# Attention tiles with tokens on partitions and DMA transposes in a fused linear-attention and two-layer kernel

## The chip, the cores and the metric

One core of one Trainium2 chip. The metric is the device time of one execution in microseconds (us). A run over 1.5% above the fastest of its kernel is marked slow. Ratios are the mean time of one kernel's fast runs over the mean of the other's fast runs of the same rounds, so they are not quite the ratio of the medians quoted.

## The reference, cut to what matters

```python
# batch 8, heads 8, seq 576, head_dim 64; d_model 512, d_ff 2048
kv  = einsum('bhsd,bhse->bhde', k, v)        # 64 x 64 per head
out = einsum('bhsd,bhde->bhse', q, kv)
x   = out / sqrt(mean(out*out, -1) + 1e-6) * g_norm   # per head; then [4608 tokens, 512]
h   = x @ w_in                                # [4608, 2048]
g   = max(h, 0) + alpha * min(h, 0)
y   = g @ w_out                               # [4608, 512]
```

The two-layer part works on nine blocks of 512 tokens, the attention on eight batches of 576.

## The kernel before: the parts that matter

Everything runs as one hand-ordered stream per engine. Block w computes the first layer of block w (64 matmuls of 512 columns in 16 groups), the second layer of block w-1 (another 64), and, between the groups, the attention of block w+1. Each head pair j takes five transposes of q on TensorE, five matmuls for kv, then:

```python
def step_ot(w, j):          # out, transposed: 128 columns of d_model x 512 tokens
    ... nc.tensor.matmul(out=ot_ps[...], lhsT=kvs[b, j][:], rhs=qts[b, j][...])
    nc.scalar.activation(out=sq[:], in_=ot_ps[:], func=AF.Square)
def ssq_mm(w, j):           # sum of squares over a head's 64 partitions: a matmul with a mask
    nc.tensor.matmul(out=ssq_ps[:], lhsT=mask16[:], rhs=sq[:])
    ... Ln, then Exp on 128 x 512, on ScalarE
def norm(w, j):             # x, transposed, ready as the moving operand of the first layer
    nc.vector.scalar_tensor_tensor(out=xts[w, j][:], in0=ot_ps[:], scalar=g2col[:], in1=rstd[:], ...)
```

Loads of a batch are issued from GpSimd (six DMAs: remainder and main part of k, v, q), and GpSimd then regroups k and q in SBUF. At block w the loads are of batch w+2, which block w+1 uses:

```python
        if 1 < w and w + 2 < B:
            load_batch(w + 2)       # at the start of block w
            regroup_batch(w + 2)
        for g in range(NF):
            m1_group(w, g)          # 4 matmuls of the first layer, Relu on ScalarE, gt on VectorE
            ...                     # 4 matmuls y of the second layer
            ...                     # some attention steps of block w + 1
```

In the profiles h_ps is the first layer, y_ps the second, qt_ps the q transposes, gt the activated values; kst, vst, qst are the staging tiles of the loads and ksb, qsb the regrouped ones. A DMA lands when its data have arrived. A PSUM bank is the buffer that a group of matmuls writes into; groups that share one take turns (at the end of block 1 of the changed kernel two groups of kv matmuls waited 0.86 and 1.06 us until VectorE had copied the one before out of their bank).

## Time and profile before

| | |
|---|---|
| time, median of 3 | 320.28 us (318.98 to 320.32) |
| span of the profiled run | 317.4 us |
| busy: TensorE / ScalarE / VectorE / GpSimd | 92% / 55% / 50% / 21% |
| granted TensorE clock | 0.993 |

A line of the profile's groups and timelines gives engine, source line, operation, out<-in, shape and count; a bracket tells how long the engine stood idle just before and what ended that. TensorE's busy time is modelled to the end of each matmul and overlaps the next (a matmul of 512 columns counts 0.379 us, and one starts every 0.216), so I measure prices and gaps from one start to the next. The lines themselves stand in the prediction below.

### The profile page before, as it was taken

To read this page: it belongs to the slowest core of one execution; us is meant where nothing else is said; L and a number is where in the kernel's file an instruction comes from. 1 tells how busy PE (TensorE), PEld (TensorE's weight loads), DVE (VectorE), ACT (ScalarE), POOL (GpSimd) and SP (SyncE) were. 2 spreads that over 40 slices of the span, in tenths; PEclk is the share of its full clock that TensorE was granted. 3 is DMA by queue.
4 is the path that set the end of the run, shared out by engine and by line. 5 is a ranking of instruction groups with operands and counts; after the bars stand their busy time and mean duration, and the time that the engine had idled before them with its cause. 6 is when DMAs were issued, how large, how long until landed. Compare 5 with 4: busy or idle time off the path is not lost.

```text
span 317.4 us, 4195 instructions
## 1 busy us (share of the span) xinstructions
PE 293.4 (92%) x1588; PEld 142.0 (45%) x1588; DVE 157.2 (50%) x267; ACT 173.4 (55%) x292; POOL 66.6 (21%) x74
## 2 busy tenths in 40 slices
PE   5668998898999999999999999999999999999994
PEld 1323453454455455545554455444544444444441
DVE  4547833666655554545464546454554445443300
ACT  2366546468466636674567456655665667444211
POOL 8434312737340541055005200000000000000000
PEclk9799999999999999999999999999999999999999
DMA  7999999998973859077715811000011111001132
GB/s 110 179 206 195 200 197 143 174 149 89 169 101 51 115 92 118 34 104 113 108 35 86 120 35 33 33 36 33 33 35 33 33 33 36 33 34 37 52 80 66
DMA packets 47621, 28.27 MB, mean 89 GB/s; under 512 B 14304, under 2 KB 42992, under 8 KB 47600
## 3 DMA queue, kind: packets, MB, share of 16 engines
q0 software_dynamic: 40320, 18.16, 45.7%
q1 hardware_dynamic: 7280, 9.84, 11.2%
q8 instruction: 12, 0.20, 0.3%
q14 instruction: 9, 0.07, 0.1%
HBM read 36.71 MB, written 9.44 MB: 145 GB/s over the span
## 4 chain that ended last, share of the span: by engine, by line
PE 85%; ACT 6%; DVE 4%; DMA 2%; issue 1%; SPq 1%; ACTq 0%
PE h_ps L323 37%; PE y_ps L345 36%; PE qt_ps L234 3%; PE kv_ps L249 3%; PE ssq_ps L287 3%; PE ot_ps L271 2%; DMA alpha_row<-in_moe_alpha_dram 2%; ACT rstd L289 2%; ACT sq_sb L277 1%; ACT rstd L292 1%; DVE gt L332 1%; DVE xt L298 1%; ACT m_sb L330 1%; SPq L100 1%; PE yb L345 1%
## 5 line engine op out<-in xcount | busy, mean ns | idle before, releaser
L332 DVE SCALAR_TENSOR_TENSOR gt<-m_sb,beta_sb,h_ps 128x512 f16<-128x512 f32 x144 | 106.8, 745 | 87.2 <-ACT m_sb L330 86.4
L323 PE MATMUL h_ps<-xt,w_in_sb 128*128 128x512 f16 x576 | 146.2, 379 | 2.9 <-DVE xt L298 1.7
L345 PE MATMUL y_ps<-w_out_sb,gt 128*128 128x512 f16 x528 | 134.8, 379 | 0.1
L330 ACT ACTIVATE m_sb<-h_ps 128x512 f32<-128x512 f32 x144 | 85.3, 594 | 80.4 <-PE h_ps L323 80.3
L345 PEld LDWEIGHTS <-gt 128*128 128x128 f16 x576 | 56.1, 98 | 67.1 <-issue 1.7
L323 PEld LDWEIGHTS <-w_in_sb 128*128 128x128 f16 x576 | 54.2, 98 | 64.2 <-issue 10.4
L298 DVE SCALAR_TENSOR_TENSOR xt<-ot_ps,g2col,rstd 128x512 f16<-128x512 f32 x36 | 27.0, 751 | 43.3 <-ACT rstd L292 43.2
L289 ACT ACTIVATE rstd<-ssq_ps,eps_t 128x512 f32<-128x512 f32 x36 | 24.7, 687 | 18.0 <-PE ssq_ps L287 17.9
L277 ACT ACTIVATE sq_sb<-ot_ps 128x512 f16<-128x512 f32 x36 | 21.3, 596 | 16.2 <-PE ot_ps L271 15.6
L352 ACT COPY y_sb<-y_ps 128x512 f32<-128x512 f32 x33 | 19.3, 586 | 18.4 <-PE y_ps L345 18.4
L292 ACT ACTIVATE rstd<-rstd 128x512 f32<-128x512 f32 x36 | 22.7, 629 | 1.1
L287 PE MATMUL ssq_ps<-sq_sb,mask 128*128 128x512 f16 x36 | 13.6, 378 | 6.7 <-ACT sq_sb L277 5.6
L129 POOL DMA_DIRECT2D vst<-in_v_dram x9 | 7.7, 860 | 50.4 <-PE kv_ps L249 48.6
L146 POOL COPY qsb<-qst 128x2048 f16<-128x2048 f16 x6 | 11.4, 1897 | 32.5 <-DMA qst<-in_q_dram 32.5
L249 PEld LDWEIGHTS <-ksb 128*128 128x128 f16 x160 | 11.6, 99 | 11.2 <-issue 4.2
L234 PE MATMUL qt_ps<-ident,qsb 128*128 128x128 f16 x160 | 14.4, 225 | 1.9 <-DVE qsb L146 1.2
L234 PEld LDWEIGHTS <-qsb 128*128 128x128 f16 x160 | 11.6, 101 | 9.4 <-DVE qsb L146 2.4
L243 DVE COPY qt_sb<-qt_ps 128x576 f16<-128x576 f16 x32 | 14.4, 451 | 2.5 <-PE qt_ps L234 2.5
L271 PE MATMUL ot_ps<-qt_sb,kv_sb 128*128 128x512 f16 (+7 forms) x64 | 13.5, 286 | 0.8 <-DVE kv_sb L257 0.7
L249 PE MATMUL kv_ps<-vst,ksb 128*128 128x128 f16 x128 | 12.3, 220 | 1.8 <-DVE qt_sb L243 1.8
L146 POOL COPY ksb<-kst 128x2048 f16<-128x2048 f16 x6 | 11.4, 1903 | 11.9 <-DMA kst<-in_k_dram 11.9
L257 DVE TENSOR_TENSOR kv_sb<-kv_ps,mask 128x128 f16<-128x128 f32 x32 | 9.0, 285 | 3.8 <-PE kv_ps L249 3.8
(43 smaller groups left out, 92.6 us busy)
## 6 DMA issues: line engine op xcount, KB each, us to landing
out_dram<-y_sb SPq DMA_DIRECT2D x40, 128.0 KB, 2.4
out_dram<-y_sb SPq DMA_DIRECT2D x16, 256.0 KB, 2.3
kst<-in_k_dram POOLq DMA_DIRECT2D x7, 512.0 KB, 6.9
qst<-in_q_dram POOLq DMA_DIRECT2D x7, 512.0 KB, 10.1
vst<-in_v_dram POOLq DMA_DIRECT2D x7, 512.0 KB, 8.4
w_in_sb<-in_moe_w_in_dram POOLq DMA_DIRECT2D x4, 512.0 KB, 14.7
w_out_sb<-in_moe_w_out_dram POOLq DMA_DIRECT2D x4, 512.0 KB, 16.1
qst<-in_q_dram POOLq DMA_DIRECT2D x2, 256.0 KB, 7.5
```

Source lines behind the costliest of these rows:

```text
L146: (eng or nc.vector).tensor_copy(out=dst, in_=src)
L234: nc.tensor.matmul(out=qt_ps[:, t * P : (t + 1) * P], lhsT=qs(t), rhs=ident16[:], is_transpose=True, start=(t == 0), stop=(t == NT - 1),)
L249: nc.tensor.matmul(out=kv_ps[:], lhsT=ks(t), rhs=vs(t), start=(t == 0), stop=(t == NT - 1),)
L277: nc.scalar.activation(out=sq[:], in_=ot_ps[:], func=AF.Square)
L287: nc.tensor.matmul(out=ssq_ps[:], lhsT=mask16[:], rhs=sq[:], start=True, stop=True)
L289: nc.scalar.activation(out=rstd[:], in_=ssq_ps[:], func=AF.Ln, bias=eps_t[:], scale=inv_d,)
L292: nc.scalar.activation(out=rstd[:], in_=rstd[:], func=AF.Exp, bias=0.0, scale=-0.5)
L298: nc.vector.scalar_tensor_tensor(out=xts[w, j][:], in0=ot_ps[:], scalar=g2col[:], in1=rstd[:], op0=ALU.mult, op1=ALU.mult,)
L323: nc.tensor.matmul(out=h_ps[:], lhsT=w_in_blk(c, g), rhs=xts[w, c][:], start=(c == 0), stop=(c == NC - 1),)
L330: nc.scalar.activation(out=m_sb[:], in_=h_ps[:], func=AF.Relu, scale=-1.0)
L332: nc.vector.scalar_tensor_tensor(out=gt[:], in0=m_sb[:], scalar=beta_sb[:, g : g + 1], in1=h_ps[:], op0=ALU.mult, op1=ALU.add,)
L345: nc.tensor.matmul(out=y[:], lhsT=gts[w, g][:, a * P : (a + 1) * P], rhs=w_out_blk(g), start=(g == 0), stop=(g == NF - 1),)
```

## The change

Its intent is to take work off TensorE. From batch 3 on, q is transposed by a DMA; the attention's output is computed with tokens on partitions, so that the sum of squares is a reduction along the free axis on VectorE rather than a matmul; each normalised row tile is transposed back by a DMA into the first layer's operand `xm`. Row tiles and their transposes stand in groups 0 to 8 of a block; loads, then q transpose and kv, stand in groups 8 to 15.

```diff
+    def transpose_q(b):
+        qtms[b] = attn_p.tile([P, NT * NPAIR, P], FP16, name="qtm")
+        nc.sync.dma_start_transpose(out=qtms[b][:], in_=bufs[b % NBUF]["q"][:]...)
+    def tile_a(b, t):      # 128 tokens: four matmuls of 128 columns, Square on ScalarE
+    def tile_b(b, t):      # sum of squares: tensor_reduce on VectorE
+    def tile_c(b, t):      # Ln, Exp on 128 x 8; rg = rstd * g_norm on GpSimd
+    def tile_d(b, t):      # x = out * rg on VectorE, then
+            nc.sync.dma_start_transpose(out=xm(w)[:, :, c : c + m], in_=x[i : i + m]...)
...
+    LOAD_G = NF // 2
     for w in range(1, NW):
-        if 1 < w and w + 2 < B:
-            load_batch(w + 2)
-            regroup_batch(w + 2)
         for g in range(NF):
+            if w > 1 and g == LOAD_G and w + 2 < B:
+                load_batch(w + 2)
+                regroup_batch(w + 2)
             m1_group(w, g)
...
+            if g == NF - 3 and w + 2 < B:
+                transpose_q(w + 2)
+            if g >= NF - NPAIR and w + 2 < B:
+                step_kv(w + 2, g - (NF - NPAIR))
```

Cut: pools, the tail of batch 2 in the old layout, the scheduling of steps.

More of the change, by code (lines that the diff above doesn't have):

```diff
@@ L48 @@
     inv_d = 1.0 / D
+    NB_PE = 3
     const_p = ctx.enter_context(tc.tile_pool(name="constp", bufs=1))
     w_p = ctx.enter_context(tc.tile_pool(name="weights", bufs=1))
-    xt_p = ctx.enter_context(tc.tile_pool(name="xt", bufs=3))
+    xt_p = ctx.enter_context(tc.tile_pool(name="xt", bufs=2))
+    xm_p = ctx.enter_context(tc.tile_pool(name="xm", bufs=3))
     qkv_p = ctx.enter_context(tc.tile_pool(name="qkv", bufs=1))
@@ L60 @@
     ps_s = ctx.enter_context(tc.tile_pool(name="pss", bufs=1, space=bass.MemoryType.PSUM))
-    ps_o = ctx.enter_context(tc.tile_pool(name="pso", bufs=2, space=bass.MemoryType.PSUM))
-    ps_q = ctx.enter_context(tc.tile_pool(name="psq", bufs=1, space=bass.MemoryType.PSUM))
+    ps_o = ctx.enter_context(tc.tile_pool(name="pso", bufs=1, space=bass.MemoryType.PSUM))
     ctx.enter_context(
@@ L104 @@
     nc.sync.dma_start(out=alpha_row[:], in_=moe_alpha[:].rearrange("(g p) -> g p", p=P))
+    g_all = const_p.tile([P, D], FP32, name="g_all")
+    nc.sync.dma_start(out=g_all[:], in_=g_norm[:].partition_broadcast(P))
     g2col = const_p.tile([P, 1], FP32, name="g2col")
@@ L260, with xt_of @@
     ots = {}
+    xms = {}
+    def xt_of(w, c):
+        return xms[w][:, c, :] if w >= NB_PE else xts[w, c][:]
     def step_ot(w, j, pool=None):
@@ L265, in step_ot @@
         else:
-            ot_ps = ps_o.tile([P, W], FP32, name="ot_ps", tag="o")
+            ot_ps = ps_o.tile([P, W], FP32, name="ot_ps", tag=f"o{j % 2}")
         n0 = w * W
@@ L285, in ssq_mm @@
         ot_ps, sq = ots.pop((w, j))
-        ssq_ps = ps_q.tile([P, W], FP32, name="ssq_ps", tag="q")
+        ssq_ps = ps_o.tile([P, W], FP32, name="ssq_ps", tag="o2")
         nc.tensor.matmul(out=ssq_ps[:], lhsT=mask16[:], rhs=sq[:], start=True, stop=True)
@@ L301, in norm, with step_tail_ot @@
         )
+    TAIL = NB_PE * (S - W)
+    JT = min(NPAIR, W // TAIL)
+    def step_tail_ot(i):
+        ot_ps = ps_o.tile([P, JT, TAIL], FP32, name="ot_ps", tag=f"o{i % 2}")
+        for u in range(JT):
+            j = i * JT + u
+            nc.tensor.matmul(
+                out=ot_ps[:, u, :], lhsT=kvs[NB_PE - 1, j][:],
+                rhs=qts[NB_PE - 1, j][:, S - TAIL : S], start=True, stop=True,
+            )
+        sq = attn_p.tile([P, JT, TAIL], FP16, name="sq_sb")
+        nc.scalar.activation(out=sq[:], in_=ot_ps[:], func=AF.Square)
+        ots["tail", i] = (ot_ps, sq)
@@ new lines, in step_tail_ssq @@
+    def step_tail_ssq(i):
+        ot_ps, sq = ots.pop(("tail", i))
+        ssq_ps = ps_o.tile([P, JT, TAIL], FP32, name="ssq_ps", tag="o2")
+        nc.tensor.matmul(out=ssq_ps[:], lhsT=mask16[:], rhs=sq[:], start=True, stop=True)
+        rstd = attn_p.tile([P, JT, TAIL], FP32, name="rstd")
+        nc.scalar.activation(
+            out=rstd[:], in_=ssq_ps[:], func=AF.Ln, bias=eps_t[:], scale=inv_d,
+        )
+        nc.scalar.activation(out=rstd[:], in_=rstd[:], func=AF.Exp, bias=0.0, scale=-0.5)
+        nc.vector.scalar_tensor_tensor(
+            out=xm(NB_PE)[:, i * JT : (i + 1) * JT, 0:TAIL], in0=ot_ps[:], scalar=g2col[:],
+            in1=rstd[:], op0=ALU.mult, op1=ALU.mult,
+        )
@@ new lines, with xm @@
+    qtms, tiles = {}, {}
+    def xm(w):
+        if w not in xms:
+            xms[w] = xm_p.tile([P, NPAIR, W], FP16, name="xm")
+        return xms[w]
+    def transpose_q(b):
+        qtms[b] = attn_p.tile([P, NT * NPAIR, P], FP16, name="qtm")
+        nc.sync.dma_start_transpose(
+            out=qtms[b][:], in_=bufs[b % NBUF]["q"][:].rearrange("p t h d -> p (t h d)"),
+        )
+    n_tile = [0]
+    def tile_a(b, t):
+        u = n_tile[0] % 4
+        n_tile[0] += 1
+        pool, tag = (ps_o, f"o{u}") if u < 3 else (ps_s, "s")
+        ot_ps = pool.tile([P, H, D], FP32, name="otm_ps", tag=tag)
+        for j in range(NPAIR):
+            nc.tensor.matmul(
+                out=ot_ps[:, 2 * j : 2 * j + 2, :], lhsT=qtms[b][:, t * NPAIR + j, :],
+                rhs=kvs[b, j][:], start=True, stop=True,
+            )
+        n = P if t < TPP else REM
+        sq = attn_p.tile([P, H, D], FP32, name="sqm_sb", tag="rstd")
+        nc.scalar.activation(out=sq[0:n], in_=ot_ps[0:n], func=AF.Square)
+        tiles[b, t] = [n, ot_ps, sq]
@@ new lines, in tile_b @@
+    def tile_b(b, t):
+        n, _, sq = tiles[b, t]
+        ss = attn_p.tile([P, H], FP32, name="ss", bufs=3)
+        nc.vector.tensor_reduce(
+            out=ss[0:n], in_=sq[0:n], op=ALU.add, axis=mybir.AxisListType.X,
+        )
+        tiles[b, t][2] = ss
+    def tile_c(b, t):
+        n, _, ss = tiles[b, t]
+        nc.scalar.activation(
+            out=ss[0:n], in_=ss[0:n], func=AF.Ln, bias=eps_t[0:n], scale=inv_d,
+        )
+        nc.scalar.activation(out=ss[0:n], in_=ss[0:n], func=AF.Exp, bias=0.0, scale=-0.5)
+        rg = attn_p.tile([P, H, D], FP32, name="rg")
+        nc.gpsimd.tensor_tensor(
+            out=rg[0:n], in0=ss[0:n].unsqueeze(2).to_broadcast([n, H, D]),
+            in1=g_all[0:n].unsqueeze(1).to_broadcast([n, H, D]), op=ALU.mult,
+        )
+        tiles[b, t][2] = rg
@@ new lines, in tile_d, with phase_steps @@
+    def tile_d(b, t):
+        n, ot_ps, rg = tiles.pop((b, t))
+        x = attn_p.tile([P, H, D], FP16, name="xrow", bufs=3)
+        nc.vector.tensor_mul(out=x[0:n], in0=ot_ps[0:n], in1=rg[0:n])
+        i = 0
+        while i < n:
+            w, c = divmod(b * S + t * P + i, W)
+            m = min(n - i, W - c)
+            nc.sync.dma_start_transpose(
+                out=xm(w)[:, :, c : c + m], in_=x[i : i + m].rearrange("p h d -> p (h d)"),
+            )
+            i += m
+    def phase_steps(w):
+        if w < NB_PE:
+            return window_steps(w)
+        if w >= NW:
+            return []
+        todo = [(b, t) for b in range(NB_PE, min(B, w + 1)) for t in range(NT)
+                if (b, t) not in done and b * S + t * P < (w + 1) * W]
+        done.update(todo)
+        steps = []
+        if w == NB_PE:
+            n = NPAIR // JT
+            for i in range(n + 1):
+                m = [lambda i=i: step_tail_ot(i)] if i < n else []
+                m += [lambda i=i: step_tail_ssq(i - 1)] if i > 0 else []
+                steps.append(m)
+            n_tile[0] = 3
+        for i in range(len(todo) + 3):
+            m = []
+            for k, fn in ((0, tile_a), (3, tile_d), (1, tile_b), (2, tile_c)):
+                if 0 <= i - k < len(todo):
+                    m.append(lambda fn=fn, x=todo[i - k]: fn(*x))
+            steps.append(m)
+        return [lambda m=m: [f() for f in m] for m in steps]
@@ L303, in window_steps @@
+    done = set()
     def window_steps(w):
@@ L323, in m1_mm @@
             nc.tensor.matmul(
-                out=h_ps[:], lhsT=w_in_blk(c, g), rhs=xts[w, c][:],
+                out=h_ps[:], lhsT=w_in_blk(c, g), rhs=xt_of(w, c),
                 start=(c == 0), stop=(c == NC - 1),
@@ L426 @@
     regroup_batch(2)
+    LOAD_G = NF // 2
     for w in range(1, NW):
-        steps = window_steps(w + 1) if w + 1 < NW else []
+        steps = phase_steps(w + 1)
         n = len(steps)
-        first_g = 4 if w == 1 else 0
-        if 1 < w and w + 2 < B:
-            load_batch(w + 2)
-            regroup_batch(w + 2)
+        g0, g1 = (4, NF - 2) if w == 1 else (0, NF // 2 + 1)
         y = None
         for g in range(NF):
-            if w == 1 and g == first_g - 1:
+            if w == 1 and g == g0 - 1:
                 load_batch(3)
                 regroup_batch(3)
+            if w > 1 and g == LOAD_G and w + 2 < B:
+                load_batch(w + 2)
+                regroup_batch(w + 2)
             m1_group(w, g)
@@ L454 @@
                     y_out(y, w - 1, a)
-            want = n * (g - first_g + 1) // (NF - 2 - first_g)
+            want = n * (g - g0 + 1) // (g1 - g0)
             while steps and n - len(steps) < want:
                 steps.pop(0)()
+            if g == NF - 3 and w + 2 < B:
+                transpose_q(w + 2)
+            if g >= NF - NPAIR and w + 2 < B:
+                step_kv(w + 2, g - (NF - NPAIR))
     for a in range(TPW):
```

## The prediction

> **What bounds the kernel now.** I read the page's busy sums and its chain first, then a table of steady stretches, then the order of time on TensorE in one of them. Page: sums, then the chain.
>
> ```profile
> PE 293.4 (92%) x1588; PEld 142.0 (45%) x1588; DVE 157.2 (50%) x267; ACT 173.4 (55%) x292; POOL 66.6 (21%) x74
> ...
> ## 4 chain that ended last, share of the span: by engine, by line
> PE 85%; ACT 6%; DVE 4%; DMA 2%; issue 1%; SPq 1%; ACTq 0%
> ```
>
> The reader is to see 85% of the chain on TensorE, with no other engine above 55% busy. A matmul's busy time overlaps its neighbour's, so next come stretches cut where a block of 512 tokens (w = 2, 3, 7) begins its first-layer matmuls; columns: stretch, length, then busy time and count of PE, PEld, DVE, ACT, POOL, the clock, DMA share, GB/s.
>
> ```profile
> 79.35:112.04 32.69, 31.92 (x182) 15.86 (x181) 17.73 (x31) 19.49 (x33) 10.33 (x9) 1.00 0.81 112
> 112.04:144.48 32.44, 31.75 (x182) 15.92 (x180) 16.86 (x29) 19.01 (x32) 8.43 (x8) 1.00 0.62 89
> ...
> 241.80:271.16 29.36, 29.36 (x138) 13.33 (x137) 14.60 (x21) 18.80 (x32) 0.00 (x0) 1.00 0.16 37
> ```
>
> TensorE is full, at full clock: it is the bound, and blocks 2 to 6 lose only 0.7 to 0.8 us. Order of time on TensorE at the end of block 3 (start, length, what, idle before):
>
> ```profile
> 138.88 1.03 PE L345 MATMUL y_ps<-w_out_sb,gt 128*128 128x512 f16 x4
> 139.75 0.38 PE L271 MATMUL ot_ps<-qt_sb,kv_sb 128*128 128x256 f16 x2
> 140.81 0.38 PE L287 MATMUL ssq_ps<-sq_sb,mask 128*128 128x512 f16 x1 [0.69 <-ACT sq_sb L277]
> 141.03 1.02 PE L323 MATMUL h_ps<-xt,w_in_sb 128*128 128x512 f16 x4
> 141.89 0.38 PE L345 MATMUL y_ps<-w_out_sb,gt 128*128 128x512 f16 x1
> ```
>
> Starts of neighbours give the price: four 512-column matmuls take 0.865 us, 0.216 each. A run of five 128-column ones starts 0.28 us before what follows it (113.76 to 114.04), 0.056 each. The gap is the one loss: the last ot started at 139.86, so from there to ssq is 0.95 us where 0.11 would do; ACT's square sits between. 0.84 us is lost in block 3, and about 4.1 us in blocks 2 to 6.
>
> Last, loads of one batch in the GpSimd queue, and medians from issue to landing:
>
> ```profile
> 72.53 0.69 POOL L135 DMA_DIRECT2D ksb<-in_k_dram  x1
> 73.20 0.89 POOL L129 DMA_DIRECT2D kst<-in_k_dram  x1
> 74.08 0.71 POOL L135 DMA_DIRECT2D vsb<-in_v_dram  x1
> 74.75 0.91 POOL L129 DMA_DIRECT2D vst<-in_v_dram  x1
> ...
> 79.72 1.90 POOL L146 COPY ksb<-kst 128x2048 f16<-128x2048 f16 x1 [2.50 <-DMA kst<-in_k_dram]
> 86.62 1.90 POOL L146 COPY qsb<-qst 128x2048 f16<-128x2048 f16 x1 [5.00 <-DMA qst<-in_q_dram]
> ```
>
> ```profile
> kst<-in_k_dram POOLq DMA_DIRECT2D x7, 512.0 KB, 6.9
> qst<-in_q_dram POOLq DMA_DIRECT2D x7, 512.0 KB, 10.1
> vst<-in_v_dram POOLq DMA_DIRECT2D x7, 512.0 KB, 8.4
> ```
>
> From the first issue: k landed after 7.2 us and was regrouped at 9.1; v is issued at +2.2 and lands 8.4 later, at +10.6; q is regrouped at +16.0 (88.52). Today this costs TensorE nothing, because a batch is loaded a whole block ahead.
>
> [...] 0.379 us busy per matmul, but a start every 0.216. [...] output stores land in 2.3 us as a median, in 6.6 us beside loads (120.59 to 127.16).
>
> **The change, part by part.** Only batches 3 to 7 and blocks 3 to 8 change.
>
> Removed from TensorE: q transposes, 5 batches x 20 x 0.056 = 5.6 us. The ot matmuls, 6 blocks x 4 x 0.216 = 5.2. The ssq matmuls, the same, 5.2. The waits for ACT's square, 4.1. Sum 20.1 us, all of it on the path.
> Added to TensorE: 25 row tiles x 4 matmuls x 0.056 = 5.6. Tail of batch 2 (192 tokens): 768 columns of ot and 768 of ssq, 0.65. Sum 6.2. The kv matmuls stay, 20 x 0.056 = 1.1 us a batch, but move one block earlier.
> Net **-13.9 us**: 306.4 if nothing new waits.
>
> ACT trades four squares and eight 128x512 Ln/Exp (7.6 us a block by 596, 687 and 629 ns) for four or five squares and tiny Ln/Exp, less in sum but packed into nine groups. DVE loses four qt copies and four scalings (4.8 us a block by 451 and 751 ns) and gains four or five reductions and products, estimated at 1.3 us a pair from the 745 ns of the like operation: 13.2 us with the gt work of nine groups, against 15.6 us of matmuls. Neither becomes the bound; half a microsecond may leak here and there. Row transposes are issued by group 8 and first read at group 16, so about 14 us hide them.
>
> **The new wait.** Loads of batch w+2 no longer start with block w, but at group 8 in program order, behind the last g-times-rstd product of GpSimd (group 7). That product needs the copy of y at group 7, Ln, Exp and itself: 0.2 + 0.6 + 0.5 + 0.9, estimated from the copies, = 2.2 us after TensorE ends group 7. The first kv stands in TensorE's order after group 12, five groups x 8 x 0.216 = 8.65 us after that point. v lands at 2.2 + 10.6 = 12.8. TensorE executes in order, so it stands for **4.2 us**, in blocks 2, 3, 4 and 5 (batches 4 to 7): 16.7 us. Batch 3 is spared: it loads at group 3 of block 1 (56.9 us), its v lands at 67.6, before its kv at about 73.
>
> q is regrouped at 2.2 + 16.0 = 18.2 us on the same clock; the block ends at 8 x 1.73 + 1.1 + 4.2 = 19.1. The transposed q is first needed in group 3 of block 3 (after about 7 us), groups 4 and 5 of the later ones. So a q transpose may take 8 us before it costs anything. [...]
>
> Sum: 320.3 - 13.9 + 16.7 = 323.1, so **323 us**: the TensorE saving is given back by loads that start too late for their first reader.
>
> **Rivals.** (a) The loads come sooner: nothing but GpSimd's own order holds them, and less other traffic could land v at +8. Then 1.6 us a block are lost, and the time is 313. Against it: the two batches with undisturbed issues landed v at 10.2 and 10.7. (b) Transposes by DMA are slow, 15 us for q: stands of 7, 5, 3.5 and 3.5 us more, 342 us; queued row transposes would also hold DVE through their three row buffers. [...] (c) ACT or DVE bound the first half of a block: at most 1 us a block by the sums, 329 at worst. (d) All hidden: 306.4, which needs both v and k within 6.4 us of issue; k alone took 7.2.
>
> **Range and chances.** The stand is 4 x (4.2 plus or minus 2) us, which gives 315 to 331; slow transposes stretch the upper end, rival (a) the lower: 312 to 335. Faster by over 2% (under 313.9) needs rival (a) at its best: 0.17. Slower by over 2% (above 326.7) needs stands of over 5.1 us or some of (b): 0.33. Within: 0.5.
>
> **What would show it.** Block 7 about 0.9 us and block 6 about 3.6 us shorter than before, with no waits for ssq: the saving is right. TensorE idle 3 to 5 us before the first kv of batches 4 to 7, released by the landing of v: the new wait is right. If that gap is ended by k's regrouping or is under 2 us, my landing times are wrong. Gaps before the row-tile matmuls, released by the q transpose, would say (b); long gaps before h_ps, released by DVE or ACT, (c). If blocks 6 and 7 are not shorter, the TensorE sum itself fails.

The sum came to 320.3 - 13.9 + 16.7 = 323.1 us: the q transpose stood in it at nothing, as hidden. Cut, where marked, are statements that no trace or run of this case shows, among them those by which I judged the length of that transpose. No run had shown one by then, so that it takes less than 8 us was an assumption; the 15 us of rival (b) and the landing at +8 of rival (a) are suppositions, too.

## The result, and the profile after

The changed kernel takes **342.22 us** (340.34 to 346.36, four runs, one of them slow); before, in the same rounds, 319.79. The ratio of fast runs is 1.068 (1.062 to 1.075): slower, and outside my range of 312 to 335. The profiled run spans 338.6 us.

The page, busy sums and chain:

```profile
PE 292.4 (86%) x1526; PEld 139.7 (41%) x1526; DVE 164.5 (49%) x275; ACT 156.8 (46%) x301; POOL 93.0 (27%) x99
...
## 4 chain that ended last, share of the span: by engine, by line
PE 53%; DMA 15%; issue 15%; POOL 8%; ACT 5%; DVE 4%; SPq 0%; POOLq 0%; ACTq 0%; DVEq 0%
```

TensorE's share of the chain fell from 85% to 53%; DMA and GpSimd have come into it, which were 2% and nothing. ("issue" is time for which the profile shows no wait, so I take the chain as a hint only.) The table of stretches, again by blocks (here w = 2, 4, 6 and 7; columns as in the prediction):

```profile
83.34:121.80 38.46, 32.59 (x170) 15.70 (x168) 17.80 (x29) 17.71 (x37) 11.57 (x11) 0.91 0.64 101
...
159.25:197.71 38.46, 31.59 (x172) 15.28 (x170) 18.63 (x31) 16.43 (x36) 13.70 (x13) 0.91 0.72 103
...
235.20:263.94 28.74, 28.74 (x151) 13.64 (x149) 17.57 (x28) 16.37 (x35) 5.20 (x5) 1.00 0.25 63
263.94:292.46 28.52, 28.52 (x145) 13.40 (x144) 16.64 (x25) 15.55 (x32) 4.17 (x4) 1.00 0.28 54
```

Blocks 6 and 7 are what the change intends: 28.74 and 28.52 us against 32.44 and 29.36, with TensorE full. Blocks 2 to 5 are 37.5 to 38.5 us against 32.4 to 32.7, and their granted clock is 0.91, not 1.00. Order of time on TensorE in block 2:

```profile
106.25 1.03 PE L475 MATMUL y_ps<-w_out_sb,gt 128*128 128x512 f16 x4
113.15 0.59 PE L252 MATMUL kv_ps<-vst,ksb 128*128 128x128 f16 x4 [5.87 <-DMA vst<-in_v_dram]
113.53 0.31 PE L252 MATMUL kv_ps<-vsb,ksb 128*128 128x128 f16 x1
113.64 1.91 PE L453 MATMUL h_ps<-xt,w_in_sb 128*128 128x512 f16 x4
115.35 1.91 PE L475 MATMUL y_ps<-w_out_sb,gt 128*128 128x512 f16 x4
```

Two things are to be seen. TensorE would have been free for the first kv at 107.1 and starts it at 113.15, on the landing of v: a stand of 6.0 us. And the four h_ps after it start 0.427 us apart (113.64 to 115.35 is 1.71 for four), double the usual 0.216: the clock has been halved (granted clock 0.50 from 111.15 to 117.97 us, and 1.00 before and after).

The same loads on GpSimd:

```profile
99.78 1.04 POOL L387 TENSOR_TENSOR rg<-ss,g_all 128x512 f32<-128x512 f32 x1 [1.35 <-ACT ss L385]
100.77 0.74 POOL L138 DMA_DIRECT2D ksb<-in_k_dram  x1
...
103.06 0.91 POOL L132 DMA_DIRECT2D vst<-in_v_dram  x1
...
109.13 1.89 POOL L149 COPY ksb<-kst 128x2048 f16<-128x2048 f16 x1 [3.61 <-DMA kst<-in_k_dram]
```

The loads begin right behind the last product of the row tiles, and k is regrouped at 111.0, so v is the later of the two. The new transposes, count and median us from issue to landing:

```profile
xm<-xrow SPq DMA_TRANSPOSE x28, 2.4
...
qtm<-qsb SPq DMA_TRANSPOSE x5, 4.1
```

A q transpose moves twenty tiles of 128x128 in one DMA. Both kinds are quick by these medians, and no gap of TensorE ahead of a row tile is put down to either.

Summed from the starts of neighbouring matmuls in the profiled run ("stand": a gap beyond the work's own time; "half clock": the excess of matmuls that start 0.427 us apart):

| us | block 2 | block 3 | block 4 | block 5 | sum |
|---|---|---|---|---|---|
| v lands after the first load issue | 12.25 | 11.58 | 13.25 | 12.45 | |
| stand before the first kv | 6.04 | 5.37 | 7.03 | 6.23 | 24.7 |
| half clock after it | 2.3 | 2.4 | 1.6 | 1.6 | 7.9 |

### The profile page after: what moved, and what is told of

It reads as the page before. It is cut to its first block, busy times and chain, and to the rows that moved or that the text cites. A ratio compares the mean times of both kernels' runs of the same rounds, so it can differ in the third digit from the quotient of the medians.

```text
span 338.6 us, 4210 instructions
## 1 busy us (share of the span) xinstructions
PE 292.4 (86%) x1526; PEld 139.7 (41%) x1526; DVE 164.5 (49%) x275; ACT 156.8 (46%) x301; POOL 93.0 (27%) x99
## 4 chain that ended last, share of the span: by engine, by line
PE 53%; DMA 15%; issue 15%; POOL 8%; ACT 5%; DVE 4%; SPq 0%; POOLq 0%; ACTq 0%; DVEq 0%
PE h_ps L453 24%; PE y_ps L475 22%; DMA vst<-in_v_dram 6%; DMA kst<-in_k_dram 4%; DMA w_in_sb<-in_moe_w_in_dram 4%; POOL rg L387 3%; PE kv_ps L252 2%; ACT rstd L296 2%; DVE gt L462 2%; ACT rstd L299 1%; DVE xt L305 1%; POOL qsb L149 1%; POOL ksb L149 1%; PE otm_ps L363 1%; ACT m_sb L460 1%
## 5 line engine op out<-in xcount | busy, mean ns | idle before, releaser
L453 PE MATMUL h_ps<-xm,w_in_sb 128*128 128x512 f16 x384 | 101.5, 388 | 0.0
L387 POOL TENSOR_TENSOR rg<-ss,g_all 128x512 f32<-128x512 f32 (+1 forms) x25 | 26.0, 1041 | 111.9 <-ACT ss L385 109.4
L453 PE MATMUL h_ps<-xt,w_in_sb 128*128 128x512 f16 x192 | 48.6, 385 | 3.0 <-DVE xt L305 1.5
L252 PE MATMUL kv_ps<-vst,ksb 128*128 128x128 f16 x128 | 13.9, 240 | 28.0 <-DMA vst<-in_v_dram 24.3
L482 ACT COPY y_sb<-y_ps 128x512 f32<-128x512 f32 x33 | 19.3, 586 | 18.8 <-PE y_ps L475 18.2
L369 ACT ACTIVATE sqm_sb<-otm_ps 128x512 f32<-128x512 f32 (+1 forms) x25 | 14.9, 597 | 8.6 <-PE otm_ps L363 8.6
L396 DVE TENSOR_TENSOR xrow<-otm_ps,rg 128x512 f16<-128x512 f32 (+1 forms) x25 | 17.0, 680 | 0.0
L375 DVE TENSOR_REDUCE ss<-sqm_sb 128x8 f32<-128x512 f32 (+1 forms) x25 | 16.9, 674 | 0.0
L305 DVE SCALAR_TENSOR_TENSOR xt<-ot_ps,g2col,rstd 128x512 f16<-128x512 f32 x12 | 9.0, 751 | 14.9 <-ACT rstd L299 14.8
L296 ACT ACTIVATE rstd<-ssq_ps,eps_t 128x512 f32<-128x512 f32 x12 | 8.2, 684 | 7.2 <-PE ssq_ps L294 7.1
L284 ACT ACTIVATE sq_sb<-ot_ps 128x512 f16<-128x512 f32 x12 | 6.9, 593 | 9.9 <-PE ot_ps L278 9.9
L363 PE MATMUL otm_ps<-kv_sb,qtm 128*128 128x128 f16 x100 | 9.7, 219 | 0.0
## 6 DMA issues: line engine op xcount, KB each, us to landing
vst<-in_v_dram POOLq DMA_DIRECT2D x7, 512.0 KB, 10.2
```

What stands on the lines that cost most here:

```text
L252: nc.tensor.matmul(out=kv_ps[:], lhsT=ks(t), rhs=vs(t), start=(t == 0), stop=(t == NT - 1),)
L296: nc.scalar.activation(out=rstd[:], in_=ssq_ps[:], func=AF.Ln, bias=eps_t[:], scale=inv_d,)
L363: nc.tensor.matmul(out=ot_ps[:, 2 * j : 2 * j + 2, :], lhsT=qtms[b][:, t * NPAIR + j, :], rhs=kvs[b, j][:], start=True, stop=True,)
L375: nc.vector.tensor_reduce(out=ss[0:n], in_=sq[0:n], op=ALU.add, axis=mybir.AxisListType.X,)
L387: nc.gpsimd.tensor_tensor(out=rg[0:n], in0=ss[0:n].unsqueeze(2).to_broadcast([n, H, D]), in1=g_all[0:n].unsqueeze(1).to_broadcast([n, H, D ...
L396: nc.vector.tensor_mul(out=x[0:n], in0=ot_ps[0:n], in1=rg[0:n])
```

## The experiments

My theory after the result: the change's saving is there, and is more than given back by k and v that land too late for their first reader, and by the half clock that each such stand brings. Rivals: the row-tile work of the first half costs the time (ScalarE, VectorE, GpSimd); the DMA transposes are slow, or slow down other transfers; the half clock costs nothing of its own.

| run | what | median us | ratio to before |
|---|---|---|---|
| before | | 319.5 | 1 |
| changed | | 342.22 | 1.068 |
| e1_ahead | loads one block earlier | 308.78 | 0.967 |
| e2_warm | dummy matmuls in the stand | 333.52 | 1.045 |
| e3_norow, e5_norow2 | no row transposes (wrong result) | 342.82, 340.92 | 1.074, 1.068 |
| e4_kvnext | kv one block later | 316.23 | 0.990 |
| e6_trim | e1 with two small losses taken out | 306.49 | 0.961 |
| e7_qpe | e1 with q transposed on TensorE | 324.34 | 1.015 |
| e8_first | e1 with loads in the first half | 329.99 | 1.035 |
| e9_qearly | e6 with q transposes at group 6 | 309.44 | 0.965 |
| e10_late | loads named at group 10 | 343.83 | 1.076 |
| e11_early | loads ahead of two row products | 323.76 | 1.013 |

(Kernels are compared only within the same rounds. All results were correct but those of e3 and e5.)

**Loads one block earlier (e1_ahead).** No buffer is added: every buffer that batch w+3 needs is already free in block w.

```diff
-            if w > 1 and g == LOAD_G and w + 2 < B:
-                load_batch(w + 2)
-                regroup_batch(w + 2)
+            if g == LOAD_G and w + 3 < B:
+                load_batch(w + 3)
+                regroup_batch(w + 3)
```

> The changed kernel with each batch's loads one block earlier (batch 4 in block 1, 5 in block 2, and so on), still at group 8. My theory (TensorE stands for late k and v before the first kv of blocks 2 to 5, 24.7 us in the changed kernel's trace, and then runs at half clock for some 4 us each time, about 7 us): both vanish, 342 - 24.7 - 7 = about 310 us. Rival, the first half of a block is what costs (DVE, ACT, or the row transposes): the time stays above 330 us, with gaps before h_ps or the row-tile matmuls. Rival, q transposes by DMA are slow: gaps before the row-tile matmuls released by qtm.

Measured: 308.78 us, 33.4 less than the changed kernel; stands and half clock in blocks 2 to 5 were 32.6 together. Blocks 2 and 3, then TensorE around the first kv of block 2:

```profile
83.83:113.90 30.07, 30.07 (x169) 14.85 (x167) 17.61 (x29) 17.69 (x37) 12.83 (x12) 1.00 0.84 121
113.90:143.54 29.64, 29.64 (x168) 14.53 (x166) 17.44 (x29) 15.55 (x33) 12.65 (x12) 1.00 0.92 135
```

```profile
106.74 1.03 PE L475 MATMUL y_ps<-w_out_sb,gt 128*128 128x512 f16 x4
107.60 0.39 PE L252 MATMUL kv_ps<-vst,ksb 128*128 128x128 f16 x4
```

TensorE is busy from edge to edge at full clock, and the gap before kv is gone. The row tiles, all DMA transposes and their places were left as they were, so the rivals of the first half and of slow transposes fall; the q transposes of blocks 2 to 4 even took 12.3 to 13.4 us here and held no row tile.

**kv one block later (e4_kvnext).** The other way to part the load from its reader:

```diff
-            if g >= NF - NPAIR and w + 2 < B:
+            if w == 1 and g >= NF - NPAIR:
                 step_kv(w + 2, g - (NF - NPAIR))
+            if w > 2 and g < NPAIR // 2 and w + 1 < B:
+                step_kv(w + 1, 2 * g)
+                step_kv(w + 1, 2 * g + 1)
```

> The changed kernel with the kv matmuls of batches 4 to 7 in groups 0 and 1 of the next block, before its row tiles; loads stay. My theory: k and v have landed by then, so no stand there; q transposed may be some 2 us late for block 3's first tile of batch 4. About 311 to 314 us. Rival, something else in blocks 2 to 5 costs the time: above 330 us.

Measured: 316.23 us, some 2 us over the expectation. The big stands are gone; what is left is new: the four kv now follow each other in two groups and share one PSUM bank, so TensorE waits for VectorE's copy (6.0 us in ten waits in the whole run), and in block 5 v was still 1.1 us late. The q transpose, which I feared, cost 0.2 us.

**Dummy matmuls in the stand (e2_warm).**

```diff
             if g >= NF - NPAIR and w + 2 < B:
+                if w > 1 and g == NF - NPAIR:
+                    keep_warm(20)
                 step_kv(w + 2, g - (NF - NPAIR))
```

> The changed kernel with 20 dummy matmuls of 512 columns (4.3 us) ahead of the first kv of blocks 2 to 5, so that TensorE computes while it waits. The loads do not move. If the half clock after each stand is a cost of its own: it vanishes and the time falls by 6 to 8 us to about 335 us, with the remaining idle time before kv at 1 to 3 us. Rival, the slow matmuls only overlap time that would be lost anyway, or the clock falls for another reason: the time stays at 342 us.

Measured: 333.52 us, 8.7 less, though the loads are as late as before and TensorE does 80 matmuls more. Block 2:

```profile
109.14 4.48 PE L207 MATMUL warm_ps<-warm,mask 128*128 128x512 f16 x20
116.55 0.38 PE L252 MATMUL kv_ps<-vst,ksb 128*128 128x128 f16 x4 [2.93 <-DMA vst<-in_v_dram]
...
116.82 1.03 PE L453 MATMUL h_ps<-xt,w_in_sb 128*128 128x512 f16 x4
```

The remaining idle time before kv was 1.2 to 3.1 us, and no matmul of blocks 2 to 5 ran at half clock. Dummies (4 x 4.3 us) and remaining idle time (7.8) are 25.1 us together, about the 24.7 of the stands before, so what fell is the half clock alone: a cost of its own of about 8 us, which follows from the idleness.

**No row transposes (e3_norow, e5_norow2).** The transposes out of `tile_d` are left out and `xm` is filled once by memset.

```diff
-            nc.sync.dma_start_transpose(out=xm(w)[:, :, c : c + m], in_=x[i : i + m]...)
```

> Gives a wrong result on purpose: the changed kernel without its row transposes (the xm tiles are filled once by memset). If row transposes that share the DMA engines are why v landed 11.6 to 13.3 us after the first load issue and not 10.6: v lands at 10.2 to 10.8, the stands fall to about 4.2 us each, total 8 us less, about 334 us, and less still if stands that short leave the clock up (327 us). Rival, the landing is late for the loads' own sake or for the stores of y: landing and time stay, 342 us.

> Gives a wrong result on purpose. The run without row transposes again, with its three memsets spread over block 0's output matmuls, where VectorE is idle: in the first form they cost some 8 us ahead of block 2. In that form v landed 10.7 to 12.1 us after the first issue (11.6 to 13.3 with the transposes) and the four stands fell from 24.7 to 19.9 us. If that holds: stands of 19 to 21 us in all, time 342 - 4 to 5 = about 337 us. Rival, the row transposes cost nothing: 342 us.

Measured: 342.82 and 340.92 us, so by time the expectation failed twice. The trace tells why: the memsets (1.76 us each on VectorE) cost as much ahead of block 2 as was spared later; from block 0's first h_ps to block 1's, e5 took 41.0 us and the changed kernel 36.1. Read by block, the expectation of e5 about holds (in e3 v landed at 10.7 to 12.1 us, not at 10.2 to 10.8): in e5 v landed 10.3, 11.5, 10.8 and 11.1 us after the first issue, 1.5 us sooner in the mean than with the transposes; the stands fell from 24.7 to 18.8, and blocks 2 to 5 from 151.9 to 146.9 us. The half clock stayed (8.9 us). So row transposes that overlap the loads explain most of the late landing, but only 4.9 of the 32.6 us that stands and half clock cost.

**Loads later, and loads earlier in the same block (e10_late, e11_early).** For a slope I moved the loads two groups down:

```diff
-    LOAD_G = NF // 2
+    LOAD_G = NF // 2 + 2
```

> The changed kernel with its loads two groups later (10 in place of 8). If the distance between the load and the first kv alone sets the stand, each of the four grows by two groups, 3.46 us, to some 9.6 us, 13.8 us in all, about 355 us, with the half clock after each as before; a little less, if fewer row transposes are in flight by then. Rival, the stand is set by something that does not move with the loads: 342 us.

Measured: 343.83 us, as the changed kernel. The experiment changed nothing: the built program has the same instructions in the same order on every engine. GpSimd does not know of groups; it issues loads when the instructions ahead of them in its own queue are done, and they began 2.3 us after group 7 as before. The run is of use as a repeat (stands of 25.7 us, half clock 9.1) and as a lesson. The next one moves the loads in that queue:

```diff
-            if w > 1 and g == LOAD_G and w + 2 < B:
+            if w > 1 and g == LOAD_G - 2 and w + 2 < B:
                 load_batch(w + 2)
+            if w > 1 and g == LOAD_G and w + 2 < B:
                 regroup_batch(w + 2)
```

> The changed kernel with the six load issues of blocks 2 to 5 placed ahead of the last two g-times-rstd products in GpSimd's order (group 6), the regroupings left at group 8. The run that named group 10 did not delay the loads: GpSimd executes in its own order and nothing there waits for a group, so they began 2.3 us after group 7 as before. This run moves them in GpSimd's order. If the distance from load to first kv sets the stand: loads begin two groups, 3.46 us, earlier, the four stands fall from 24.7 to about 11 us in all, each under 4 us, and the half clock after them (7.9 us) mostly goes: 342 - 14 - 8 = 320 us, 323 if the loads now meet more row transposes. Rival, late row products (behind 4.5 us of issues on GpSimd) hold VectorE and TensorE in the first half: gaps before h_ps, 330 us or more.

Measured: 323.76 us. Block 2:

```profile
106.12 1.02 PE L453 MATMUL h_ps<-xt,w_in_sb 128*128 128x512 f16 x4 [0.81 <-DVE gt L462]
...
112.07 0.38 PE L252 MATMUL kv_ps<-vst,ksb 128*128 128x128 f16 x4 [2.34 <-DMA vst<-in_v_dram]
...
112.35 1.03 PE L453 MATMUL h_ps<-xt,w_in_sb 128*128 128x512 f16 x4
```

The stands before kv fell by four us a block (8.7 in all), the half clock vanished, and v landed 12.0 to 13.1 us after the first issue, where the changed kernel had 11.6 to 13.3. The rival is seen too, but small: a gap of about 0.9 us a block ahead of an h_ps, as a row product came late to VectorE. Distance from load to reader sets the stand.

**Loads in the first half (e8_first).** e1 with the loads of blocks 2 to 4 at group 0:

```diff
-            if g == LOAD_G and w + 3 < B:
+            if (g == 0 if w > 1 else g == LOAD_G) and w + 3 < B:
```

> The earlier-load kernel with loads and regroupings at group 0 of blocks 2 to 4 in place of group 8 (batches 5 to 7), that is beside the row transposes. GpSimd executes in order, so the g-times-rstd products of the row tiles stand behind the regroupings, which wait some 15 us for q: VectorE stands in the row products, then h_ps is not freed and TensorE stands. I expect 5 to 10 us more for each of three blocks, 324 to 340 us. Rival, halves do not matter once loads are early: 309 us.

Measured: 329.99 us. VectorE, then TensorE, in block 2:

```profile
109.75 0.69 DVE L396 TENSOR_TENSOR xrow<-otm_ps,rg 128x512 f16<-128x512 f32 x1 [10.65 <-POOL rg L387]
```

```profile
111.74 1.87 PE L453 MATMUL h_ps<-xt,w_in_sb 128*128 128x512 f16 x4 [8.11 <-DVE gt L462]
```

The chain is as expected: GpSimd waits for q to regroup it, the row product waits for GpSimd (10.65 us), VectorE executes in order and does not free h_ps, and TensorE stands for 8.3 us, then runs at half clock. Blocks 2 to 4 lost 15.8 us to stands and 6.0 to half clock (the stand of block 3, 2.3 us, was ended by ScalarE's copy of y). That is what the halves of the change protect; the second half is the right place for loads, a block earlier.

**q on TensorE again (e7_qpe).** e1 with `step_t` for batches 3 to 7 in place of the DMA transpose of q.

```diff
-        nc.sync.dma_start_transpose(out=qtms[b][:], in_=bufs[b % NBUF]["q"][:]...)
+            if NF - 2 * NPAIR <= g < NF - NPAIR and w + 2 < B and w > 1:
+                step_t(w + 2, g - (NF - 2 * NPAIR))
+            if w == 1 and g >= NF - NPAIR:
+                step_t(w + 2, g - (NF - NPAIR))
```

Cut: `tile_a` reads q from the tile of `step_t`.

> The earlier-load kernel with q transposed by TensorE again (20 matmuls of 128 columns and four VectorE copies a batch), row tiles and row transposes kept: what the DMA transposes of q are worth. TensorE is the bound there, so 5 x 1.12 us more in all, about 314.5 us, and up to 3 us beyond that in block 1, where kv and transposes share a PSUM bank. Rival, the DMA transposes of q hinder as much as they spare: 309 us or less.

Measured: 324.34 us, far more than expected, for a reason of my own making: in block 1 transposes and kv of batch 3 share one PSUM bank in the same groups (kv waited 1.29, 2.31, 0.88 and 1.34 us for the copies of q out of it), and block 1 took 37.1 us rather than 27.7 (about 2.8 us of that by half clock). Blocks 2 to 5, which are clean, took 124.3 us against 119.2: 5.1 us for four batches, 1.28 each, where 1.12 was expected. So DMA transposes of q do spare TensorE its transposes' time; the total time of this run says nothing.

**Two smaller losses (e6_trim).** e1, with the load of `g_norm` moved behind block 0, and three of batch 3's four kv moved from the end of block 1 into groups 0 to 2 of block 2.

```diff
-            if g >= NF - NPAIR and w + 2 < B:
+            if w == 1 and g == NF - 1:
+                step_kv(w + 2, 0)
+            if w > 1 and g >= NF - NPAIR and w + 2 < B:
                 step_kv(w + 2, g - (NF - NPAIR))
+            if w == 2 and g < NPAIR - 1:
+                step_kv(w + 1, g + 1)
```

Cut: the move of the `g_norm` load, and the PSUM bank of the first row tile (`n_tile[0]` from 3 to 0).

> The earlier-load kernel (308.8 us) with two smaller losses taken out: the load of g_norm over 128 partitions moved behind block 0 (the first-layer matmuls began 1.0 to 1.4 us later than before the change), and three of batch 3's four kv moved into block 2, where each has the PSUM bank to itself (TensorE waited 0.86 and 1.06 us for it at the end of block 1). Both right: about 306 us. If neither was a cost: 309 us.

Measured: 306.49 us, the lowest median; 0.961 of the kernel before. Its interval (0.957 to 0.966) overlaps that of e1 (0.965 to 0.969), so a gain over e1 is not clear. The kv part was right: block 1 fell from 27.7 to 25.0 us, 0.84 of that being work that moved. The `g_norm` part was wrong: block 0 does not begin earlier. A new gap appeared in block 3, so that blocks 1 to 7 took 203.8 us in the trace, against 204.2 in e1's:

```profile
122.30 0.40 PE L362 MATMUL otm_ps<-kv_sb,qtm 128*128 128x128 f16 x4 [1.34 <-DMA qtm<-qsb]
```

Here the q transpose is issued beside loads, and took 13 to 14.5 us in blocks 2 to 4 rather than 4.1.

**q transposes at group 6 (e9_qearly).** e6 with

```diff
-            if g == NF - 3 and w + 2 < B:
+            if g == (NF - 3 if w == 1 else 6) and w + 2 < B:
```

> The trimmed kernel (306.5 us) with the q transposes of blocks 2 to 5 issued at group 6 in place of 13. There q was regrouped a block ago, and no loads are in flight: beside them a q transpose took 12 to 14.5 us, alone 4.1, and the late one of block 2 held a row tile of block 3 for 1.5 us. If so: q transposes land in 4 to 6 us, no gap before the row-tile matmuls, about 305 us. Rival, q in the way of the row transposes at group 6 costs as much: 306.5 us or more.

Measured: 309.44 us (306.8 to 309.7), ratio 0.965 with an interval of 0.961 to 0.970 that overlaps e6's (0.957 to 0.966): not better. The q transposes took 5.7 to 8.1 us and the gap in block 3 is gone, but block 5's first h_ps now waits 1.5 us for a row transpose, which stood behind q and beside loads. The rival was right.

## Why the prediction was wrong

The bound and the saving were right. Traces of the kernel before and of e1 differ by 15.3 us over blocks 2 to 7 (191.8 against 176.5), and batch 3's kv add 1.1 to block 1: 14.2 net, where I had 13.9.

The new wait was right in kind and place: the first kv of batches 4 to 7, ended by the landing of v, as I wrote. Its size was not. **The first step that failed is "v lands at 2.2 + 10.6 = 12.8".** The loads began 2.29 us after group 7 in all four blocks, so that term held; but v landed 12.4 us after the first issue in the mean. I had taken medians of a kernel with no transposes on the DMA engines. Row transposes of the last tiles were still in flight then, and took up to 9 us themselves; without them v came at 10.9 (e5). The stand was 6.2 us in the mean, not 4.2: 8.0 us in four blocks. What the last 0.3 us of the landing is owed to stays open.

**The second failure is a term that is not in the sum at all**: what TensorE's clock does after a stand. It added 7.9 us; I had counted a stand at its length alone. In the changed kernel the granted clock was 0.50 for 6.83 us at each of the four stands, of which part fell within the stand itself. The trace of the kernel before shows no such case: after its first 20 us no wait of TensorE was longer than 1.1 us, and the clock was 1.00 until 316.4 us, 1.0 us before the end. Over all runs the clock stayed after gaps of 2.5 (e11, block 2) and 3.1 us (e2, block 2), and halved after every one of 4.1 us or more (e5, block 2, is the shortest). But length alone does not decide: after gaps of 2.3 us (e8, block 3), 2.5 us (e7, block 1) and 2.8 us (e5, block 0) it halved as well. That of e8 (four matmuls from 144.87 on take 1.62 us, not 0.865):

```profile
140.82 1.03 PE L453 MATMUL h_ps<-xm,w_in_sb 128*128 128x512 f16 x4
144.00 1.02 PE L475 MATMUL y_ps<-w_out_sb,gt 128*128 128x512 f16 x4 [2.16 <-ACT y_sb L482]
144.87 1.83 PE L453 MATMUL h_ps<-xm,w_in_sb 128*128 128x512 f16 x4
```

The traces show what does. Within each, the changes of the clock lie multiples of 3.41 us apart. I cut all thirteen traces at these places into stretches of 3.41 us, from 30 us on and without the end of the run. 23 stretches at full clock had 2.13 us or more in sum without a busy matmul: after each of them the clock was half. The other 957 had 1.90 us or less: after each of them it stayed full. (In the changed kernel the four ahead of the half clock had 2.58 to 3.41 us, the others 1.09 us at most.) So short gaps in one stretch add up, a gap that is split between two stretches may pass, as those of e11 and e2 did, and one of over some 4.3 us, twice 2.13, should not (an estimate from these figures). No run moved a gap within a stretch to test this.

I also missed 1.9 us in block 1, where kv of batches 2 and 3 wait for one PSUM bank (the e6 run removed them). Block 1 begins 1.0 us later than in the trace before; e6 showed that the `g_norm` load is not the reason, and it stays open.

The sum of the profiled runs, against a difference of 21.2 us: -14.2 (TensorE) + 24.7 (stands) + 7.9 (half clock) + 1.9 (PSUM bank) + 1.0 (later start) = 21.3.

Of the rivals, (a), loads that come sooner, failed: they came later. (b), slow transposes, named 342 us, which is what was measured, but it was not the cause: q landed in 4.1 us where I had allowed 8, and no row tile waited for it. A number that comes out right is no proof of its story. (c) failed with e1. (d), all hidden at 306.4, is nearly what the mended kernels reach.

## What to carry to other kernels

When work is moved to an earlier place in a bound engine's order, its inputs' loads must move with it: take the distance from load to first reader, in the bound engine's time, and compare it with a landing measured beside the traffic that the new kernel will have (here v at 12.4 us in the mean, not at 10.6). In these runs every stand of TensorE of 4.1 us or more cost half clock on top of its own length, 1.6 to 2.4 us each in the changed kernel, and so did some shorter gaps, from 2.3 us on, and several that came to 2.13 us or more within one stretch of 3.41 us: count the first, and take the others as a risk. And on GpSimd "at group 8" meant only "behind what stands ahead of it": naming group 10 instead left the order, and the time, as they were (e10, 343.83 us).
